# A fused dynamic convolution and two feed-forward blocks: the head of the program rebuilt, with small unread matmuls in planned waits

## The chip, the core and the metric

The kernel runs on one core of one Trainium2 chip. The metric is the device time of one execution in microseconds (us). A core has five engines with a queue each: PE (TensorE, matrix products into PSUM), ACT (ScalarE), DVE (VectorE), POOL (GpSimd, which has no access to PSUM here) and SP (SyncE, which issues all the DMAs of this kernel). PSUM has eight banks of 512 float32 columns.

## What is computed

The input x has 2 batches of 4160 tokens with 192 features. Three steps follow each other:

```python
w = softmax(weight_gen, axis=-1)                # (2, 4160, 8 heads, 7 taps)
att[b, s, h] = sum_k w[b, s, h, k] * x_pad[b, s + k, h]      # causal, 7 rows of x

xk, xr = mu_k * att + (1 - mu_k) * prev(att), mu_r * att + (1 - mu_r) * prev(att)
y = sigmoid(xr @ w_r) * (relu(xk @ w_k) ** 2 @ w_v)          # d_ff = 1024

h = relu(y @ w_in)
c = conv_w[0] * h[s - 1] + conv_w[1] * h[s] + conv_w[2] * h[s + 1]
out = (h * sigmoid(c)) @ w_out
```

Several weights arrive as float64 and are narrowed to float32 on the chip.

## The kernel before, in words

**Tiles.** Each batch is cut into ten tiles of tokens: 256, 220, seven of 476, and 352. The two batches (b0, b1) of a tile are worked side by side. Everything below runs per tile i and batch b.

**Stages of a tile.** `attention` (line 468) loads overlapping rows of x with one DMA per batch, multiplies 7 rows by the softmax weights in one 128x1344 product per token slot (2 slots per batch in tiles 0 and 1, 4 in the full ones), and sums the seven parts: with PE into a `pa` bank in tile 0 (`total`, line 486), with three POOL adds in the others. All these products run on POOL. The sums go to `tok`. `mixing` (line 509) transposes `tok` on PE and makes xk and xr, each as a high and a low part. Unit u=0 makes features 0 to 127 of b0, u=1 those of b1, and u=2 the remaining 64 features of both batches at once; u=2 sends its parts to `xB` by eight DMAs from SBUF to SBUF (lines 567, 568) and needs both batches. `moe1` (line 608) makes one of eight 128-wide chunks of the first block: five matmuls into a `pa` bank, ReLU, square and a cast on ACT, a subtraction on DVE, and later five more matmuls (`out_passes`) into the accumulators `am` and `ar`. `gate_r` makes the sigmoid gate, `mix_out` multiplies by it and writes `x2`. `moe2` does the second block in the same manner (`pc` bank, tapped convolution on ACT and DVE, accumulators `bm` and `br`), 12 steps behind `moe1`; tiles 0 and 1 are handled together in it, as one unit of 476 tokens.

**Weights.** `prepare` (line 416) fetches sixteen chunks of weights through a ring of three `stage` buffers and narrows each (`narrow`, line 337): an ACT copy with a scale into bank `bm` or `br`, four DVE instructions, two matmuls that add the float32 parts, and then a split into high and low parts by two ACT casts with a matmul between. The narrowed value and its power of two use two rings of banks, `px_r` (`bm`, `br`) and `py_r` (the two `pc` banks).

**Softmax.** Tile 0, tile 1, tile 2 and the rest are four groups (`softmax`, line 437): DVE reduces and inverts, ACT takes the exponential, and the two broadcast passes (subtract the maximum, multiply by the inverse) run on DVE for tile 0 and on POOL for the others.

**Order.** Every instruction is first recorded with a planned time `now` (`at(t, ...)`), which is a priority. `Program.schedule` (line 114) then goes through all of them with a table of costs (`cost`, line 84), always gives the next free engine the ready instruction with the lowest `now`, and emits everything in the order of the planned starts. Each engine's queue is in that order on the chip; waits between engines are by semaphores on the real data. SP's queue is planned in the same way, and a DMA whose buffer isn't free holds up the DMAs behind it. `hold` is a planned time before which an instruction isn't placed: the row loads of tile 1 have 25.0 and 33.0.

Of the kernel before, what the change touches and what calls it, by code (L numbers as in the profile page):

```python
# [16 lines left out]
SIZES = [256, 220] + [476] * 7 + [352]  # L17
# [25 lines left out]
class Program:  # L43
# [40 lines left out]
    def cost(self, eng, method, out, ins, pointer):  # L84
# [3 lines left out]
        if method == "dma_start":  # L88
            return 0.6, 0.0
# [24 lines left out]
    def schedule(self):  # L114
# [4 lines left out]
        for i, (eng, method, a, k, _, hold) in enumerate(self.ops):  # L119
# [38 lines left out]
        for _ in range(n):  # L158
# [39 lines left out]
def conv_moe_kernel(ctx: ExitStack, tc: tile.TileContext, xp, wg_first, wg_rest, mus, w_k, w_v, w_r, w_in, conv_w, w_out, out):  # L198
# [90 lines left out]
    py_r = Ring(pc_r.tiles)  # L289
# [5 lines left out]
    omt_r = Grow(om_r.tiles, (SPARE, [spare[:, 5 * W:6 * W]]))  # L295
    pt_r = Grow(pc_r.tiles, (16 * NTILE, pa_r.tiles))
# [40 lines left out]
    def narrow(st, n):  # L337
# [5 lines left out]
        ACT.activation(px, f(hi), ACTF.Copy, scale=2.0 ** -112)  # L343
        if on_pe[0]:

            zr = wz_r()[:, :n]
            DVE.tensor_scalar(x, x, 3, None, op0=ALU.logical_shift_left)
            DVE.scalar_tensor_tensor(out=z, in0=hi, scalar=0x80000000, in1=x, op0=ALU.bitwise_and, op1=ALU.bitwise_or)
# [4 lines left out]
            return px  # L353
        DVE.tensor_scalar(x, x, 3, None, op0=ALU.logical_shift_left)
# [82 lines left out]
    def softmax(j, a, b, eng, times, bank):  # L437
# [3 lines left out]
        if bank is not None:  # L441
            z = bank[:, :n * NH].rearrange("p (s h) -> p s h", s=n)
# [25 lines left out]
    def attention(i, b, t_load, t, dt_, eng, hold=(0.0, 0.0)):  # L468
# [7 lines left out]
        def token(l):  # L476
# [7 lines left out]
            if i < 1:  # L484

                def total():
# [3 lines left out]
                    ACT.copy(tok_t[i][:, l, b * DM:b * DM + DM], z)  # L490
# [18 lines left out]
    def mixing(i, u, t, dt_):  # L509
# [5 lines left out]
        def flip():  # L515
# [408 lines left out]
```

## Time and profile before

| | |
|---|---|
| median of 3 runs | 742.6 us (742.06 to 743.72) |
| the profiled execution, its own time | 743.48 us |
| its span in the profile | 741.7 us, so 1.8 us lie outside the span |
| busy share: PE, weight loads, ACT, DVE, POOL | 96%, 82%, 88%, 78%, 74% |
| granted TensorE clock, mean | 0.992 of full speed |

Times in the rows are in us from the start of the span unless marked ns; PEld is PE's loading of weights, SPq SP's queue. All recorded instructions carry line 183, where the schedule emits them, so they are told apart by the names of their tiles: `prod` is a product of the convolution, `pa` the bank of a first matmul, `s` the hidden values, `am` and `ar` the accumulators, `stage` raw weights (and, late, scratch), `sw` the softmax weights.

### The profile page before, as it was taken

The page shows a single profiled execution, that of the slowest core. Times are in us where ns is not written, and L with a number is a line of the kernel's source. Part 1 is how long each engine was busy: PE and PEld are TensorE (multiplying, and loading weights), DVE is VectorE, ACT ScalarE, POOL GpSimd, SP SyncE. Part 2 cuts the span into 40 slices and gives each one's busy share as a digit, 9 for nine tenths or more (in the row PEclk, how much of TensorE's full clock was granted, in tenths as well). Part 3 has the DMA queues.
Part 4 walks back from the last instruction along what each step waited for, and adds up shares of the span by engine and source line. Part 5 has one row for each costly group of instructions (what it writes and reads, how often), then busy time and mean ns, then how long its engine had stood idle before and what let it go on. Part 6 is the DMA issues. An engine that isn't in the chain of part 4 may idle for free.

```text
span 741.7 us, 10552 instructions
## 1 busy us (share of the span) xinstructions
PE 708.9 (96%) x3473; PEld 606.4 (82%) x3473; DVE 579.6 (78%) x985; ACT 653.6 (88%) x1388; POOL 547.0 (74%) x398
## 2 busy tenths in 40 slices
PE   3898988999999999999999999999999999999996
PEld 2776777888788888888888888888888888899995
DVE  5666977888898978797879787978796858686775
ACT  2588788999999999898989898989898989899986
POOL 3798999999799999999999999999013423242333
PEclk9899999999999999999999999999999999999999
DMA  7678203021310230212112302120002000200000
GB/s 223 172 219 258 97 1 106 1 74 53 73 54 20 82 93 7 73 47 81 53 27 74 101 1 68 61 61 1 20 5 69 0 21 0 60 2 21 1 21 30
DMA packets 18791, 45.09 MB, mean 61 GB/s; under 512 B 2992, under 2 KB 14256, under 8 KB 18608
## 3 DMA queue, kind: packets, MB, share of 16 engines
q1 hardware_dynamic: 18736, 44.41, 20.1%
q8 instruction: 27, 0.44, 0.3%
q14 instruction: 28, 0.23, 0.1%
HBM read 27.40 MB, written 6.39 MB: 46 GB/s over the span
## 4 chain that ended last, share of the span: by engine, by line
PE 80%; POOL 8%; ACT 5%; issue 3%; DVE 2%; DMA 1%; SPq 0%; POOLq 0%; ACTq 0%; DVEq 0%
PE pa L183 25%; PE pc L183 18%; PE bm L183 12%; PE am L183 11%; PE br L183 7%; PE ar L183 7%; POOL prod L183 5%; ACT pa L183 1%; DMA stage<-in_moe_w_k_dram 1%; POOL s L183 1%; ACT L183 1%; DVE stage L183 0%; POOL g L183 0%; POOL xA L183 0%; POOL tok L183 0%
## 5 line engine op out<-in xcount | busy, mean ns | idle before, releaser
L183 DVE SCALAR_TENSOR_TENSOR pc<-h,cw,pc 128x476 f32<-128x476 f32 (+1 forms) x276 | 194.4, 704 | 42.2 <-ACT pc L183 39.3
L183 POOL TENSOR_TENSOR prod<-rows,sw 128x1344 f32<-128x1344 f32 x70 | 216.5, 3094 | 13.5 <-DMA stage<-in_moe_w_v_dram 10.9
L183 ACT ACTIVATE pa<-pa 128x476 f32<-128x476 f32 (+4 forms) x326 | 163.9, 504 | 38.0 <-PE pa L183 33.6
L183 POOL TENSOR_TENSOR prod<-prod 128x576 f32<-128x576 f32 (+1 forms) x132 | 161.5, 1224 | 9.6
L183 PE MATMUL am<-s,wv 128*128 128x476 f32 (+3 forms) x480 | 141.8, 356 | 0.9 <-ACT s L183 0.9
L183 PE MATMUL bm<-g,wo 128*128 128x476 f32 (+1 forms) x411 | 133.6, 379 | 1.1 <-ACT g L183 0.8
L183 PE MATMUL pa<-xA,wkA 128*128 128x476 f32 (+3 forms) x480 | 123.6, 363 | 5.2 <-DVE ar L183 2.5
L183 POOL TENSOR_TENSOR g<-stage,g 128x476 fp32r<-128x476 f32 (+1 forms) x41 | 47.5, 1158 | 97.5 <-ACT g L183 93.6
L183 DVE TENSOR_TENSOR s<-pa,s 128x476 fp32r<-128x476 f32 (+3 forms) x160 | 93.9, 587 | 27.8 <-ACT s L183 27.1
L183 PE MATMUL pc<-x,wiA 128*128 128x478 f32 (+1 forms) x414 | 112.0, 376 | 0.0
L183 PE MATMUL ar<-s,wv 128*128 128x476 f32 (+3 forms) x320 | 108.9, 354 | 0.2 <-DVE x L183 0.2
L183 PE MATMUL br<-g,wo 128*128 128x476 f32 (+1 forms) x274 | 102.3, 375 | 0.0
L183 PEld LDWEIGHTS pa<-xA,wkA 128*128 128x128 f32 x480 | 83.4, 190 | 23.1 <-DVE s L183 6.7
L183 PEld LDWEIGHTS am<-s,wv 128*128 128x128 f32 x480 | 86.8, 188 | 12.8 <-ACT s L183 2.1
L183 ACT ACTIVATE pc<-h,cw 128x476 f32<-128x476 f32 (+1 forms) x138 | 92.0, 667 | 1.2
L183 PE MATMUL pa<-xB,wkB 128*128 128x476 f32 (+3 forms) x320 | 88.7, 357 | 0.0
L183 PEld LDWEIGHTS bm<-g,wo 128*128 128x128 f32 x411 | 76.2, 189 | 12.6 <-ACT g L183 1.6
L183 DVE TENSOR_TENSOR pc<-h,pc 128x476 f32<-128x476 f32 x96 | 62.8, 654 | 29.8 <-ACT pc L183 29.4
L183 PEld LDWEIGHTS pc<-x,wiA 128*128 128x128 f32 x414 | 75.6, 189 | 11.8 <-DVE g L183 2.0
L183 ACT CAST s<-pa 128x476 fp32r<-128x476 f32 (+3 forms) x160 | 82.3, 516 | 1.9
L183 ACT ACTIVATE h<-pc 128x478 f32<-128x478 f32 (+1 forms) x138 | 78.9, 572 | 5.5 <-PE pc L183 4.5
L183 PE MATMUL pc<-x,wiB 128*128 128x478 f32 (+1 forms) x276 | 81.4, 375 | 0.0
(147 smaller groups left out, 1170.6 us busy)
## 6 DMA issues: line engine op xcount, KB each, us to landing
rows<-in_x_dram SPq DMA_DIRECT2D x14, 960.0 KB, 4.7
xB<-rm SPq DMA_DIRECT2D x28, 119.0 KB, 2.3
rows<-in_x_dram SPq DMA_DIRECT2D x4, 768.0 KB, 6.9
xB<-mk SPq DMA_DIRECT2D x16, 119.0 KB, 2.3
rows<-in_x_dram SPq DMA_DIRECT2D x2, 864.0 KB, 4.4
out_dram<-stage SPq DMA_DIRECT2D x7, 238.0 KB, 2.0
out_dram<-om SPq DMA_DIRECT2D x7, 238.0 KB, 2.2
stage<-in_moe_w_v_dram SPq DMA_DIRECT2D x4, 384.0 KB, 4.3
```

Source lines behind the costliest of these rows:

```text
L183: getattr(self.real[eng], method)(*a, **k)
```

## The change

Only the head, up to the first full tile, is rebuilt; tiles 2 to 9 keep their code.

1. Tiles 0 and 1 become 238 tokens each instead of 256 and 220, so two chunks of one tile fit side by side in one bank (2 x 238 = 476 columns). `moe1_half`, `gate_half` and `mix_out_half` do for tiles 0 and 1 two chunks (or both feature halves) in one instruction on ACT and DVE. The matmuls stay one per chunk and pass.
2. In tile 0 the two products of b0 move from POOL to DVE, with an earlier time; those of b1 stay on POOL. The softmax of tile 1 and tile 2 moves from POOL to DVE, that of tile 1 before the weights; the maximum and the sum of the first three groups are kept in bank `am`.
3. `tok` of tile 0 also holds the last 64 features twice (one more ACT copy per slot). New mixing units 5 and 6, one per batch, transpose that doubled block and write `xB` in place, so unit 2 and its eight DMAs go in tile 0, and b0 no longer waits for b1.
4. `narrow` gets its sign from a parametric ReLU on ACT instead of an AND/OR on DVE: three DVE instructions instead of four, in all sixteen chunks.
5. `py_r` has one bank; the other `pc` bank is lent to the `pa` ring (three banks) up to planned time 26.
6. The plan prices a DMA's issue at 0.45 us (0.6 before), its bandwidth at 310 GB/s (240), its landing at 0.75 us (0.8), and takes the exponential's table as loaded. The row loads of tile 1 are held to 8.0 and 16.0 instead of 25.0 and 33.0.
7. Where PE waits in the plan between 2.5 and 48.0 us, the schedule puts 32-column matmuls (signs times signs) into columns 480 to 511 of bank `am`, one per 0.11 us of planned wait, until 0.15 us before the next real matmul. Nobody reads them.

```diff
-SIZES = [256, 220] + [476] * 7 + [352]
+SIZES = [238, 238] + [476] * 7 + [352]
+WARM = 2.5, 48.0
@@ cost / schedule
-            return 0.6, 0.0
+            return 0.45, 0.0
...
+        done = WARM[0]
         for i in sorted(range(n), key=lambda i: (start[i], i)):
             eng, method, a, k = self.ops[i][:4]
+            if eng == "PE":
+                while done < start[i] - 0.15 and start[i] < WARM[1]:
+                    self.idle(done == WARM[0])
+                    done += 0.11
+                done = start[i] + dur[i]
             getattr(self.real[eng], method)(*a, **k)
@@ banks
-    py_r = Ring(pc_r.tiles)
+    py_r = Ring(pc_r.tiles[:1])
...
+    LENT = 26
+    pa_r = Lend(LENT, pa_r.tiles + pc_r.tiles[1:], pa_r)
@@ narrow
-        ACT.activation(px, f(hi), ACTF.Copy, scale=2.0 ** -112)
...
-            DVE.tensor_scalar(x, x, 3, None, op0=ALU.logical_shift_left)
-            DVE.scalar_tensor_tensor(out=z, in0=hi, scalar=0x80000000, in1=x, op0=ALU.bitwise_and, op1=ALU.bitwise_or)
+            ACT.activation(px, f(hi), ACTF.Prelu, scale=2.0 ** -112, alpha=-(2.0 ** 32))
+            DVE.tensor_scalar(z, x, 3, None, op0=ALU.logical_shift_left)
@@ softmax
-            z = bank[:, :n * NH].rearrange("p (s h) -> p s h", s=n)
+            m, z = (bank[:, k * n * NH:(k + 1) * n * NH].rearrange("p (s h) -> p s h", s=n) for k in (0, 1))
@@ attention, tile 0
-                    ACT.copy(tok_t[i][:, l, b * DM:b * DM + DM], z)
+                    x = tok_t[i][:, :, b * DM:b * DM + DM]
+                    m, r = 64 * b, 128 - 128 * b
+                    ACT.copy(x[:, l, m:m + 128], z[:, m:m + 128])
+                    ACT.copy(x[:, L + l, 0:128].rearrange("p (k d) -> p k d", k=2), z[:, r:r + 64].unsqueeze(1).to_broadcast([128, 2, 64]))
@@ mixing
+            elif u > 4:
+                x = xB_r[k]()
+                xin[i, u - 5, k, 1] = x
+                x = x.unsqueeze(1)
...
+            if u > 4:
+                h = slice(64, 128)
+                (POOL if i else DVE).tensor_tensor(x[h, 0, :N], st[k][h, :N], f(x[h, 0, :N]), op=ALU.subtract)
+                return
@@ moe1_half (gate_half and mix_out_half are built alike)
+        def go():
+            st["p"] = pa_r()[:, :2 * N]
+            for j, p in enumerate(halves(st["p"], N)):
+                mm(p, passes_in(wkA, wkB, xin[i, b, 0, 0], xin[i, b, 0, 1], slice(128 * (fi + j), 128 * (fi + j) + 128), N))
+        def c1():
+            ACT.activation(st["p"], st["p"], ACTF.Relu)
...
+        def go2():
+            m, r = halves(HALF[b], N)
+            for j in range(2):
+                out_passes(wv, fi + j, st["s"][:, :, j * N:j * N + N], N, m, r, one=True)
@@ the plan
-    attention(0, 0, -100.1, -90, 0.1, POOL)
+    attention(0, 0, -100.1, -94.3, 0.05, DVE)
...
-    softmax(1, 0, slots[1], POOL, (-83.85, -83.65, -83.64, -83.63, -83.62, -83.55), am_r.tiles[0])
+    softmax(1, 0, slots[1], DVE, (-92, -91.9, -91.8, -91.7, -91.6, -91.5), am_r.tiles[0])
...
-    softmax(2, 0, slots[2], POOL, (0.9, 0.91, 0.92, 0.93, 0.94, 0.95), None)
+    softmax(2, 0, slots[2], DVE, (0.9, 0.91, 0.92, 0.93, 0.94, 0.95), am_r.tiles[0])
...
-    mixing(0, 2, -75, 0.1)
-    mixing(0, 1, -70, 0.1)
+    mixing(0, 5, -87, 0.1)
+    mixing(0, 1, -75, 0.1)
+    mixing(0, 6, -74, 0.1)
...
+    prog.idle = lambda first: nc.tensor.matmul(am_r.tiles[0][:, 480:512], lhsT=signs[:, 0:128], rhs=signs[:, 0:32], start=first, stop=True, skip_group_check=True)
```

## Rows read from the trace of the kernel before

**Rows 1.** Busy time of each engine by stretches, granted clock, DMA:

```profile
core 0: us, PE busy (x) PEld busy (x) DVE busy (x) ACT busy (x) POOL busy (x), PEclk, DMA share, GB/s
11.20:32.00 20.80, 19.08 (x79) 14.65 (x79) 14.06 (x29) 8.78 (x24) 15.53 (x8) 1.00 0.71 193
32.00:60.00 28.00, 23.24 (x123) 17.89 (x124) 20.43 (x43) 22.42 (x65) 24.94 (x19) 0.88 0.68 207
60.00:80.00 20.00, 17.61 (x112) 14.05 (x112) 13.18 (x33) 16.10 (x49) 17.96 (x15) 1.00 0.72 208
80.00:100.00 20.00, 17.32 (x127) 15.25 (x126) 17.06 (x35) 16.25 (x58) 19.37 (x14) 1.00 0.14 51
100.00:124.80 24.80, 21.37 (x128) 17.99 (x126) 19.65 (x34) 21.33 (x45) 22.92 (x19) 1.00 0.20 60
124.80:130.00 5.20, 5.20 (x17) 4.42 (x18) 3.25 (x7) 4.45 (x11) 5.04 (x4) 0.67 0.43 94
200.00:273.00 73.00, 73.00 (x343) 61.98 (x343) 65.16 (x109) 68.35 (x139) 70.49 (x48) 1.00 0.17 51
...
32.00:40.00 8.00, 5.59 (x16) 3.68 (x16) 7.08 (x17) 5.49 (x17) 7.76 (x6) 0.57 0.35 84
```

**Rows 2.** The timeline of PE, first complete chunk of tile 2:

```profile
124.78 1.34 PE L183 MATMUL pa<-xA,wkA 128*128 128x476 f32 x3 [0.44 <-ACT r L183]
```

**Rows 3.** The timeline of POOL: start, us, instruction, idle before:

```profile
12.29 6.04 POOL L183 TENSOR_TENSOR prod<-rows,sw 128x1344 f32<-128x1344 f32 x2 [10.94 <-DMA stage<-in_moe_w_v_dram]
...
32.02 3.03 POOL L183 TENSOR_TENSOR prod<-rows,sw 128x1344 f32<-128x1344 f32 x1
...
114.76 2.37 POOL L183 TENSOR_TENSOR xA<-stage,xA 128x476 fp32r<-128x476 f32 x2
```

**Rows 4.** The timeline of DVE around the first softmax:

```profile
5.21 0.55 DVE L183 TENSOR_REDUCE h<-sw 128x32 f32<-128x224 f32 x1 [4.32 <-DMA sw<-in_first_dram]
...
7.01 0.56 DVE L183 TENSOR_REDUCE am<-sw 128x32 f32<-128x224 f32 x1 [0.46 <-ACT sw L183]
...
10.25 0.19 DVE L183 TENSOR_SCALAR am<-am 128x32 f32<-128x32 f32 x1
...
10.98 0.35 DVE L183 RECIPROCAL h<-am 128x32 f32<-128x32 f32 x1
...
11.83 0.37 DVE L183 TENSOR_TENSOR sw<-sw,h 128x224 f32<-128x224 f32 x1
```

**Rows 5.** SP's queue: row loads of tile 0's b1 and tile 1's b0:

```profile
3.97 0.43 SPq L183 DMA_DIRECT2D rows<-in_x_dram  x1
...
21.40 1.21 SPq L183 DMA_DIRECT2D rows<-in_x_dram  x1
```

**Rows 6.** DMA issues, count, KB each, median us to landing:

```profile
rows<-in_x_dram SPq DMA_DIRECT2D x4, 768.0 KB, 6.9
```

**Rows 7.** Groups of instructions up to 200 us on ACT: busy, mean ns of one:

```profile
L183 ACT ACTIVATE pa<-pa 128x476 f32<-128x476 f32 x36 | 19.8, 556 | 1.1 <-PE pa L183 0.8
L183 ACT ACTIVATE pa<-pa 128x256 f32<-128x256 f32 x32 | 12.1, 383 | 4.9 <-PE pa L183 4.6
L183 ACT ACTIVATE pa<-pa 128x220 f32<-128x220 f32 x32 | 11.0, 344 | 3.9 <-PE pa L183 3.5
```

**Rows 8.** Groups of DVE instructions, the same view over the whole span:

```profile
L183 DVE TENSOR_TENSOR g<-pc,g 128x476 fp32r<-128x476 f32 x96 | 62.3, 649 | 10.7 <-ACT g L183 10.6
...
L183 DVE SCALAR_TENSOR_TENSOR stage<-stage,br 128x384 uint32<-128x384 uint32 x5 | 2.7, 549 | 0.1
```

**Rows 9.** Two equal DVE instructions, and what POOL ran beside the second:

```profile
29.93 0.20 DVE L183 TENSOR_SCALAR h<-h 128x64 f32<-128x64 f32 x1
...
192.66 0.71 DVE L183 TENSOR_SCALAR stage<-stage 128x64 f32<-128x64 f32 x1
...
192.12 1.20 POOL L183 TENSOR_TENSOR stage<-stage,rm 128x476 fp32r<-128x476 f32 x1
```

**Rows 10.** The timeline of ACT, one of its four table loads up to 125 us:

```profile
52.78 1.28 ACT L183 ACT_TABLE_LOAD   x1
```

More of the change, by code (lines that the diff above doesn't have):

```diff
@@ L33 @@
 S_LAG, G_LAG = 3.25, 4.75
+S_LAG_HALF, HSTEP = 3.25, 1
+HEAD = {(i, b): 16 * i + 8 * b for i in range(2) for b in range(2)}
 DONE = 16 * NTILE + S_LAG - 0.95
@@ L174, in schedule @@
                 wires[eng] = max(wires[eng], t + dur[i] + 0.6) + moved[i]
-                end = wires[eng] + 0.8
+                end = wires[eng] + 0.75
             for j in succ[i]:
@@ L295, in conv_moe_kernel, with __init__, __call__ @@
     omt_r = Grow(om_r.tiles, (SPARE, [spare[:, 5 * W:6 * W]]))
+    class Lend:
+        def __init__(self, until, first, then):
+            self.until, self.first, self.then = until, Ring(first), then
+        def __call__(self):
+            return self.first() if prog.now < self.until else self.then()
+    LENT = 26
+    pa_r = Lend(LENT, pa_r.tiles + pc_r.tiles[1:], pa_r)
+    pa_r.tiles = pa_r.then.tiles
     pt_r = Grow(pc_r.tiles, (16 * NTILE, pa_r.tiles))
@@ L582, in conv_moe_kernel @@
     r_t = {}
+    HALF = [am_r.tiles[0], ar_r.tiles[0]]
     acc = {}
@@ L644, in moe1, with halves, gate_half, sg @@
         at(t + S_LAG, go2)
-    def out_passes(W, fi, s, n, am, ar):
+    def halves(bank, n):
+        return bank[:, 0:n], bank[:, n:2 * n]
+    def gate_half(i, b, t):
+        N = SIZES[i]
+        st = {}
+        def go():
+            st["p"] = pa_r()[:, :2 * N]
+            for k, p in enumerate(halves(st["p"], N)):
+                mm(p, passes_in(wrA, wrB, xin[i, b, 1, 0], xin[i, b, 1, 1], slice(128 * k, 128 * k + 128), N))
+        def sg():
+            r_t[b, "half"] = r_r[b]()[:, :2 * N]
+            ACT.activation(r_t[b, "half"], st["p"], ACTF.Sigmoid)
+        at(t, go)
+        at(t + 0.3, sg)
@@ new lines, in mix_out_half, with d0, a0, d2 @@
+    def mix_out_half(i, b, t):
+        N = SIZES[i]
+        X = x2[b]
+        c = slice(OFFSET[i] + 2, OFFSET[i] + N + 2)
+        both = HALF[b][:, :2 * N]
+        m, r = halves(both, N)
+        def d0():
+            DVE.tensor_tensor(both, r_t[b, "half"], both, op=ALU.mult)
+        def a0():
+            ACT.copy(X[0:64, 3, c], r[0:64])
+            ACT.copy(X[:, 0:3:2, c], both.rearrange("p (k n) -> p k n", k=2))
+        def d2():
+            DVE.tensor_tensor(X[64:128, 3, c], r[0:64], f(X[0:64, 2, c]), op=ALU.subtract)
+            DVE.tensor_tensor(X[:, 1, c], m, f(X[:, 0, c]), op=ALU.subtract)
+        at(t, d0)
+        at(t + 0.15, a0)
+        at(t + 0.4, d2)
@@ L843, in conv_moe_kernel @@
             carry(i, b, t + 7)
-            for k in range(2):
-                gate_r(i, b, k, t + 5.12 + k)
-            for fi in range(NF):
-                moe1(i, b, fi, t + fi)
-                if i:
+            if i < 2:
+                h = HEAD[i, b]
+                gate_half(i, b, h + 5.12 * HSTEP)
+                for fi in range(0, NF, 2):
+                    moe1_half(i, b, fi, h + HSTEP * fi)
+                mix_out_half(i, b, h + S_LAG_HALF + 6 * HSTEP + 0.27)
+            else:
+                for k in range(2):
+                    gate_r(i, b, k, t + 5.12 + k)
+                for fi in range(NF):
+                    moe1(i, b, fi, t + fi)
+                mix_out(i, b, t + S_LAG + 7.27)
+            if i:
+                for fi in range(NF):
                     moe2(i, b, fi, t + fi + LAG)
-            mix_out(i, b, t + S_LAG + 7.27)
             if i:
```

46 lines of the change are left out of this document (34 added, 12 removed).

## The prediction

> **What bounds the kernel now.** I read the busy times by stretches first. From 200 to 273 us PE is busy for all 73.00 of 73 us [rows 1], and the page's slices say the same up to the last one. Past about 130 us the end is therefore set by PE's queue alone: a microsecond of PE's idle time that is saved earlier comes off the end, and nothing else does. Before that PE waits. It begins at 11.2 us, and from there to 124.8 us its busy time falls short of the span in every stretch: by 1.7, 4.8, 2.4, 2.7 and 3.4 us, 15.0 us together [rows 1]. There are hidden losses too: from 32 to 40 us the granted clock is 0.57, so a good part of these 8 us went at the lower of the two levels (1.2 instead of 2.4 GHz), with PE busy for only 5.59 of them; and from 80 to 100 us PE handled 127 matmuls against 128 in the following 24.8 us, of which many are twice as wide [rows 1], so short matmuls stand apart there.
>
> Next, who holds PE up. The chain of waits lies on POOL's products without a break until tile 2 is summed, and POOL's timeline tells why: its first product starts at 12.29, tile 1's first at 32.02, and the last sum of tile 2 is done when its subtraction starts at 114.76 [rows 3]. From there it is 10.0 us of mixing, casts and DMAs to the first complete chunk of tile 2 on PE at 124.78 [rows 2]. After that PE waits for POOL no more: its busy time is full although POOL's own, 70.49 of 73, is not [rows 1].
>
> **The change part by part.**
>
> *POOL's start.* Between 12.29 and 32.02 POOL did four products of tile 0 and the softmax passes of tiles 1 and 2. Two products and the four passes leave it. What remains is two products at 3.02 us, half of the 6.04 of the pair [rows 3], so 6.0 us. They need the softmax and b1's rows. The softmax of tile 0 starts at 5.21 and has its sum at 7.57; the three instructions left (0.19, 0.35, 0.37 us) ended only at 12.20, since the weight chunk's shifts stood between them [rows 4]. With the softmax first they end at about 7.57 + 0.91 + three gaps of 0.1 = 8.8. The rows of b1 were issued at 3.97 [rows 5] and land after about 6.9 [rows 6], at 10.9.
>
> *The products of b0 on DVE.* No row shows a 128x1344 product there. Of tensor-tensor instructions on DVE, 224 columns take 0.37 [rows 4] and 476 take 0.65 us [rows 8], so 1.1 ns a column and about 1.6 us for 1344; POOL's 3.02 is the upper bound. I take 1.6: done at 8.8 + 3.2 = 12.0. DVE and POOL read SBUF at once then, and a row bears on it: the same 128x64 instruction took 0.20 us with POOL idle and 0.71 us when a POOL subtraction ran from 192.12 to 193.32, and it ended as that ended [rows 9].
>
> By that row POOL's first product of b1 waits for DVE's second, to 12.0 instead of 10.9, or DVE's second waits up to 3.0 us for POOL. The Trainium skill ("SBUF — State Buffer", "Who interferes with whom") says that a VectorE instruction with two SBUF inputs and a GpSimd instruction that reads SBUF exclude each other for whole instructions; by that rule POOL starts at 12.0, without it at 10.9. The softmax passes that move have their second input in PSUM, so only these two products are concerned.
>
> I take 12.0, and POOL is free at 18.0. Tile 1 also needs its own softmax, seven instructions like those above, 3 to 4 us once its weights are there, so about 16, and its rows. Their load was issued at 21.40 [rows 5]; with the smaller hold it can go when b0's products free the buffer at 12.0, and lands by 12.4 + 6.9 = 19.3 at the latest, 17 if the wires are free. I take 18.5 for tile 1's first product instead of 32.02: **13.5 us earlier**. Bounds: 17.0 (no lock, rows in time) gives 15; if the load isn't issued before 21.40 since SP stands at a weight fetch whose buffer is taken, it lands at 28 and the gain is 4. Loads that go earlier pass in front of the fetches of w_k and w_v and of the copies to wkB, which lose the wire time of one row load, 3 to 4 us; these chunks are needed when the products' mixing is through, some 25 us, so they have room.
>
> *POOL from tile 1 to tile 2.* Nothing else changes on POOL: 82.7 us from 32.02 to 114.76, of which some 4 are waits. Tile 2 is then summed at 101.2, and its first chunk can start at 111.3 if the 10.0 us behind it stay.
>
> *Can the others keep up?* PE must have done by 111.3 what it had done by 124.8. That has to come out of its idle 15.0 us and the clock; so ACT, DVE and the banks decide. For tiles 0 and 1 ACT did 32 chunks, with two passes and a cast each: 48 instructions of 0.383 and 48 of 0.344 [rows 7], 34.9 us. It now does 16 pairs with three at 0.556, 26.7 us: 8.2 less. Gates and `mix_out` save 1 to 2 us more. Eight added instructions in tile 0 (copies, shifts, casts) cost at most 8 x 0.38 = 3.1. The parametric ReLU replaces a copy one for one. ACT's 84.9 us from 11.2 to 124.8 become about 78, in 100 us: 78%, against 94% from 200 to 273 us [rows 1]. DVE loses nine sign instructions of 0.55 us [rows 8] and six wider ones, 9 us in all, saves 3 on the pairs, and gets 3.2 for products, 2 for softmax passes and 2 for the fourth mixing unit: 5 us less. A pair holds its bank for one round of ACT and DVE where two chunks had two, and there are three banks at first. The matmuls stay as many, with as many columns. SP loses eight DMAs, and b0 of tile 0 no longer waits for b1's products, so `moe1` of tile 0 starts earlier. So I cost the pace at nothing; the cover is ACT's free 22%.
>
> *The unread matmuls.* In planned waits they cost nothing, and PE's queue is in order, so they run while the wait for real data goes on. Below: the stretch from 32 to 40 us at 0.57 [rows 1] lost up to 8 x 0.43 = 3.4 us, and a chain that passes through it is shortened by some of that. Above: of the 11.2 us before PE's first matmul 8.7 lie behind 2.5, and some 4 more of waits follow up to 48 us; at 0.11 us each that is about 115 matmuls, 12.7 us, if all of them fell on work. I take zero, the nearer end, as the waits are waits for others. The stretch at 0.67 from 124.8 to 130 us [rows 1] lies beyond them.
>
> *Sum.* The profiled execution took 743.5 us, 0.9 above the median of the runs shown. 743.5 - 13.5 = 730.0; against the median 742.6 it is **729.1 us**.
>
> **The rivals.**
>
> *The pace binds (0.18).* POOL is early, but the narrowing of sixteen chunks, two banks at a time, and ACT hold PE. For it: ACT was busy 80% and more from 32 to 60 us [rows 1] with PE waiting. Against it: the ACT and DVE savings above. Then only the slow clock's 3.4 us and some 3 us of bank waits go: 736.
>
> *More than POOL's shift (0.14).* Pairs also close the idle 3.4 us before 124.8, 2.7 of 80 to 100, and 1.7 of the slow 5.2 us behind it [rows 1]: 13.5 + 7.8, so 721.3.
>
> *No change (0.06).* The row load stays late and PE's idle time only moves: 742.
>
> *The unread matmuls tie PE to DVE (0.08), slower.* They write bank `am`, in which the first three softmax groups now keep their maxima and sums, and their place in the queues is that of the plan, whose DMA prices are lower than the 6.9 us of the rows [rows 6]. If a matmul that waits for late weights stands ahead of them, every softmax instruction on that bank waits behind it on DVE, and POOL behind that. With softmax 1 done at 23 instead of 16, 6.5 us are lost, and with all 12.7 us on work: 729.1 + 19.2 = 748.3. It decides from 13.5 us of such losses on.
>
> *The parametric ReLU needs a table of its own (0.03), slower.* No row shows the function. A load takes 1.28 us [rows 10]; to and fro for sixteen chunks is 32 loads, 41 us, of which ACT's idle time up to 100 us hides 25 and its savings 7; with POOL's gain lost, 743.5 + 9 = 752. The Trainium skill ("ScalarE: Activation LUTs", "Table sets: the hidden batching unit") says that cheap functions are in every set as filler, and doesn't name this one; by it there are no loads.
>
> **How the numbers follow.** The forecast has 0.51. About 0.2% (1.5 us) is what a measurement of this kernel can tell from no change. Faster by more: 0.51 + 0.18 + 0.14 = 0.83; within: 0.06; slower: 0.08 + 0.03 = 0.11. The forecast's own bounds (gains of 4 and 15) give 727.6 to 738.6. The range takes in both faster rivals and half of no change, 717 to 742, which leaves out the slower cases and a tail below, under 0.2.
>
> **What would show it.** Right: POOL's first product of tile 1 at 17 to 20 us, the last of tile 2 done by 99 to 103, first complete 476-column chunk on PE at 109 to 113; two DVE products of about 1.6 us before 13 us; table loads still four up to that chunk; ACT's hidden-layer passes 476 wide; granted clock at 1.00 from 30 to 48 us. Wrong: the row load of tile 1 still issued past 20 us; POOL early but PE idle in front of ACT; softmax instructions on DVE that wait for PE; or PE's real matmuls queued behind unread ones.

## The result and the profile after

The changed kernel takes **749.5 us** (median of 5 runs, 748.91 to 754.32) beside 742.6 us of the kernel before (741.96 to 744.3): a ratio of 1.0111, 95% interval 1.0091 to 1.0131. The forecast was 729.1 us, within 717 to 742. So the sign is wrong, and the distance is 20.4 us. The profiled execution of the changed kernel is its longest run, 754.32 us; a second one, near the median, comes with the experiments (e12).

Busy time by stretches, as in [rows 1], of the changed kernel, whose span is 752.5 us:

```profile
core 0: us, PE busy (x) PEld busy (x) DVE busy (x) ACT busy (x) POOL busy (x), PEclk, DMA share, GB/s
0.00:11.20 11.20, 5.13 (x25) 5.17 (x25) 6.14 (x12) 3.45 (x6) 0.75 (x7) 1.00 0.80 247
11.20:32.00 20.80, 20.23 (x95) 18.23 (x96) 11.88 (x26) 8.52 (x26) 11.06 (x5) 1.00 0.54 180
32.00:60.00 28.00, 26.51 (x161) 22.29 (x162) 20.07 (x39) 20.87 (x55) 22.95 (x17) 0.88 0.58 185
60.00:80.00 20.00, 16.32 (x112) 13.79 (x112) 10.31 (x23) 14.59 (x37) 14.68 (x13) 0.95 0.78 220
80.00:100.00 20.00, 19.28 (x141) 18.46 (x140) 15.85 (x26) 16.27 (x41) 18.05 (x13) 0.88 0.20 70
100.00:124.80 24.80, 18.65 (x97) 15.75 (x97) 17.15 (x28) 15.62 (x30) 20.57 (x16) 0.93 0.11 41
200.00:273.00 73.00, 69.15 (x315) 58.13 (x315) 62.98 (x105) 62.45 (x128) 66.31 (x45) 0.98 0.19 54
```

PE is busier than before up to 60 us, 51.9 of 60 instead of 42.3 (13.9 us of it are unread matmuls), and yet no further: it falls short by 3.7 us from 60 to 80 (2.4 before), by 6.2 from 100 to 124.8 (3.4 before), and by 3.9 from 200 to 273, where the kernel before lost nothing.

The timeline of PE at the start; line L979 is the unread matmul, L194 the list schedule that issues everything else:

```profile
6.07 8.26 PE L979 MATMUL am<-signs 128*128 128x32 f32 x38 [6.07 <-DVE sw L194]
14.16 7.63 PE L194 MATMUL pa<-prod,ident 128*128 128x192 f32 x28
```

The first 38 unread matmuls stand in front of the first sums of tile 0's products. They can't begin before DVE's softmax has left bank `am`, at 6.07, and they take 8.26 us, 0.217 each where the plan prices 0.11. The 28 sums behind them then take 7.63 us: the first 18 start 0.32 us apart, the last ten 0.16. In the same trace and those of the experiments 14 of these sums take 2.44 us, 0.17 each, when they run later. So 8 us of 32-column matmuls haven't brought PE to the faster pace. It begins at 19.9 us, where the trace's first record of the granted clock stands, at the higher of the two levels (2.4 instead of 1.2 GHz); before that record the PEclk column reads 1.00 only because nothing is recorded.

The group of the unread matmuls in the whole span, busy time, mean ns of one, and idle time before them:

```profile
L979 PE MATMUL am<-signs 128*128 128x32 f32 x80 | 15.1, 326 | 8.1 <-DVE sw L194 6.4 <-DVE am L194 1.7
```

The timeline of DVE in the first 27 us:

```profile
5.53 0.39 DVE L194 TENSOR_TENSOR sw<-sw,am 128x224 f32<-128x224 f32 x1
...
7.69 3.03 DVE L194 TENSOR_TENSOR prod<-rows,sw 128x1344 f32<-128x1344 f32 x2
...
14.36 0.56 DVE L194 TENSOR_REDUCE am<-sw 128x32 f32<-128x224 f32 x1 [0.39 <-PE am L979]
...
23.40 0.47 DVE L194 SCALAR_TENSOR_TENSOR ar<-pc,mu,att 128x238 f32<-128x238 f32 x1 [7.60 <-ACT att L194]
...
26.07 0.38 DVE L194 TENSOR_TENSOR sw<-sw,am 128x224 f32<-128x224 f32 x1
```

Softmax 0 is done at 5.92 and the two products of b0 at 10.7. Softmax 1 begins at 14.36 but ends only at 26.45: from 15.8 on its sum stands behind a mixing instruction (`ar`), which waits 7.60 us for ACT, which waits for the sums on PE. The exponential that the softmax's sum needs stands on ACT behind the copies of the same PE sums, too, and runs only at 23.27.

The timeline of POOL, as in [rows 3]:

```profile
19.08 6.04 POOL L194 TENSOR_TENSOR prod<-rows,sw 128x1344 f32<-128x1344 f32 x2 [17.73 <-PE pa L194]
26.83 3.04 POOL L194 TENSOR_TENSOR prod<-rows,sw 128x1344 f32<-128x1344 f32 x1 [1.71 <-PE pa L194]
...
56.21 0.69 POOL L194 TENSOR_TENSOR xA<-mk,xA 128x238 fp32r<-128x238 f32 x1 [4.27 <-ACT xA L194]
...
116.68 2.37 POOL L194 TENSOR_TENSOR xA<-stage,xA 128x476 fp32r<-128x476 f32 x2
```

There are two product buffers. DVE fills both, and POOL's first product waits until PE has summed one: 19.08, not 12.29. Tile 1's first product comes 5.2 us earlier than before, and all of it is given back on the way to tile 2, which is summed at 116.68 instead of 114.76.

### The profile page after: what moved, and what is told of

Same layout as the page of the kernel before. It is cut to its first block, busy times and chain, and to the rows that moved or that the text cites. A ratio compares the mean times of both kernels' runs of the same rounds, so it can differ in the third digit from the quotient of the medians.

```text
span 752.5 us, 10602 instructions
## 1 busy us (share of the span) xinstructions
PE 721.4 (96%) x3555; PEld 624.2 (83%) x3555; DVE 578.7 (77%) x959; ACT 649.2 (86%) x1340; POOL 537.6 (71%) x392
## 4 chain that ended last, share of the span: by engine, by line
PE 86%; ACT 5%; DVE 3%; issue 2%; POOL 1%; DMA 1%; POOLq 0%; ACTq 0%; DVEq 0%
PE pa L194 26%; PE pc L194 19%; PE bm L194 12%; PE am L194 12%; PE br L194 8%; PE ar L194 8%; PE am L979 2%; DVE stage L194 1%; POOL s L194 1%; ACT pc L194 1%; ACT pa L194 1%; ACT x L194 1%; DVE pc L194 1%; DVE am L194 1%; DMA stage<-in_moe_w_out_dram 1%
## 5 line engine op out<-in xcount | busy, mean ns | idle before, releaser
L194 DVE SCALAR_TENSOR_TENSOR pc<-h,cw,pc 128x476 f32<-128x476 f32 (+1 forms) x276 | 194.4, 705 | 45.3 <-ACT pc L194 42.4
L194 POOL TENSOR_TENSOR prod<-rows,sw 128x1344 f32<-128x1344 f32 x68 | 210.2, 3091 | 19.8 <-PE pa L194 19.4
L194 ACT ACTIVATE pa<-pa 128x476 f32<-128x476 f32 (+2 forms) x284 | 153.2, 540 | 32.2 <-PE pa L194 28.3
L194 POOL TENSOR_TENSOR prod<-prod 128x576 f32<-128x576 f32 (+1 forms) x132 | 161.5, 1224 | 9.3
L194 PE MATMUL bm<-g,wo 128*128 128x476 f32 (+1 forms) x411 | 134.7, 379 | 7.5 <-ACT g L194 7.2
L194 PE MATMUL am<-s,wv 128*128 128x476 f32 (+2 forms) x464 | 134.1, 357 | 0.0
L194 PE MATMUL pa<-xA,wkA 128*128 128x476 f32 (+2 forms) x450 | 119.4, 370 | 0.6 <-ACT r L194 0.4
L194 POOL TENSOR_TENSOR g<-stage,g 128x476 fp32r<-128x476 f32 (+1 forms) x41 | 47.5, 1159 | 97.5 <-ACT g L194 93.6
L194 PE MATMUL pc<-x,wiA 128*128 128x478 f32 (+1 forms) x414 | 113.5, 380 | 0.7 <-ACT x L194 0.7
L194 PE MATMUL ar<-s,wv 128*128 128x476 f32 (+2 forms) x336 | 106.1, 355 | 2.9 <-ACT s L194 2.8
L194 PE MATMUL br<-g,wo 128*128 128x476 f32 (+1 forms) x274 | 103.3, 378 | 2.1 <-DVE stage L194 2.1
L194 DVE TENSOR_TENSOR s<-pa,s 128x476 fp32r<-128x476 f32 (+1 forms) x139 | 88.2, 634 | 17.9 <-ACT s L194 17.4
L194 PEld LDWEIGHTS pa<-xA,wkA 128*128 128x128 f32 x450 | 81.0, 193 | 17.0 <-DVE s L194 3.0
L194 ACT ACTIVATE pc<-h,cw 128x476 f32<-128x476 f32 (+1 forms) x138 | 92.1, 668 | 1.3
L194 PEld LDWEIGHTS bm<-g,wo 128*128 128x128 f32 x411 | 76.7, 189 | 19.3 <-ACT g L194 8.6
L194 PEld LDWEIGHTS am<-s,wv 128*128 128x128 f32 x464 | 81.8, 189 | 10.3 <-DVE x L194 0.3
L194 ACT ACTIVATE h<-pc 128x478 f32<-128x478 f32 (+1 forms) x138 | 79.0, 572 | 13.1 <-PE pc L194 12.2
L194 PEld LDWEIGHTS pc<-x,wiA 128*128 128x128 f32 x414 | 76.0, 190 | 13.2 <-DVE g L194 2.7
L194 DVE TENSOR_TENSOR pc<-h,pc 128x476 f32<-128x476 f32 x96 | 62.7, 653 | 31.5 <-ACT pc L194 31.3
L194 ACT ACTIVATE pc<-pc 128x476 f32<-128x476 f32 (+1 forms) x148 | 81.1, 548 | 5.3 <-DVE pc L194 2.3
L194 PE MATMUL pa<-xB,wkB 128*128 128x476 f32 (+2 forms) x300 | 85.2, 364 | 0.0
L194 PE MATMUL pc<-x,wiB 128*128 128x478 f32 (+1 forms) x276 | 81.7, 376 | 0.0
```

## The experiments

All times are medians; the kernel before took 742.3 to 742.7 us beside them. The ledger that the experiments lead to is the sum PE busy + PE idle = span, from the first line of each profile. The spans are those of the profiled executions, which lie up to 1.4 us off the medians beside them (e9 above its median by that much), so differences of 1 us between rows say little:

| kernel | time, us | span | PE busy | of it unread | idle | tile 2 summed on POOL |
|---|---|---|---|---|---|---|
| before | 742.6 | 741.7 | 708.9 | 0 | 32.8 | 114.76 |
| e9, front alone | 741.6 | 741.2 | 707.6 | 0 | 33.6 | 106.30 |
| e3, all but unread matmuls and prices | 736.1 | 733.7 | 706.6 | 0 | 27.1 | 104.14 |
| e1, all but unread matmuls | 738.9 | 737.1 | 703.0 | 0 | 34.1 | 105.00 |
| e12, the changed kernel | 748.5 | 746.7 | 717.4 | 15.7 | 29.3 | 114.66 |
| e13, e3 with 34 unread matmuls | 735.4 | 733.1 | 705.8 | 6.0 | 27.3 | 105.80 |

### e1: no unread matmuls

```diff
-WARM = 2.5, 48.0
+WARM = 2.5, 0.0
```

> The changed kernel without its unread matmuls; order and everything else as it is. Theory A (the 80 unread matmuls hold up PE's queue in the head: the first 38 ran from 6.07 to 14.3 us at 0.217 us each, though the first product was there at about 9.2): PE's first product sum starts at 9 to 10 us, POOL's first product at 13 to 15 instead of 19.08, POOL's first product of tile 1 at 20 to 22 instead of 26.83, and the time falls by 5 to 12 us, to 737 to 744. Rival B (the new order as such is what the chip does badly, with DVE, ACT and POOL queues that wait in the wrong place): the time stays at 746 or more, and POOL still waits some 10 us in tiles 1 and 2.

738.88 us (736.32 to 739.31), ratio 0.9947, interval 0.9933 to 0.996. Its first product sum and its POOL:

```profile
8.32 6.84 PE L194 MATMUL pa<-prod,ident 128*128 128x192 f32 x28 [8.32 <-DVE prod L194]
```

```profile
12.98 6.05 POOL L194 TENSOR_TENSOR prod<-rows,sw 128x1344 f32<-128x1344 f32 x2 [11.62 <-DMA stage<-in_moe_w_v_dram]
20.19 3.06 POOL L194 TENSOR_TENSOR prod<-rows,sw 128x1344 f32<-128x1344 f32 x1 [1.16 <-PE pa L194]
...
105.00 2.38 POOL L194 TENSOR_TENSOR xA<-stage,xA 128x476 fp32r<-128x476 f32 x2
```

The unread matmuls cost 749.5 - 738.9 = 10.6 us and make the sign. Without them the sums start 5.8 us earlier and POOL is where the prediction had it within 2 to 4 us: tile 1 at 20.2 (forecast 18.5), tile 2 summed at 105.0 (forecast 101.2), 9.8 earlier than before. But the time is only 3.4 us shorter than the 742.29 beside it. That is the second question.

### e2: unread matmuls in the kernel before

```diff
+WARM = 2.5, 48.0
...
+            if eng == "PE":
+                while done < start[i] - 0.15 and start[i] < WARM[1]:
+                    self.idle(done == WARM[0])
+                    done += 0.11
```

> The kernel before with the same rule for unread matmuls in its own planned waits up to 48 us (its plan gives 146 of them, 71 ahead of the first real matmul), nothing else changed. Theory A: 71 x 0.217 us can't all fit before 11.2 us, PE's first real matmul comes 5 to 15 us later, and the time rises by 5 to 15 us, to 748 to 758. Rival B: they run in real waits and cost under 3 us, 741 to 746.

762.55 us (762.31 to 763.42), ratio 1.0271, interval 1.0255 to 1.0287: 20.3 us, more than the 5 to 15 expected. The timeline of PE:

```profile
11.21 15.30 PE L867 MATMUL am<-signs 128*128 128x32 f32 x71 [11.21 <-DVE h L191]
26.35 2.05 PE L191 MATMUL bm<-stage,ident 128*128 128x512 f32 x2
```

Here 71 of 146 stand in front of the first real matmul, which starts at 26.35 instead of 11.2, 15.1 of the 20.3 us. They take the planned wait twice: once while they wait for DVE themselves, and once again as work.

### e3: the old prices in the plan, no unread matmuls

```diff
-            return 0.45, 0.0
+            return 0.6, 0.0
...
-        port, table = 0.0, ACTF.Exp
+        port, table = 0.0, None
```

(and a DMA's 310e3 back to 240e3, 0.75 to 0.8, and `WARM` as in e1).

> The changed kernel without its unread matmuls and with the old prices of DMAs and the exponential's table in the plan (0.6, 240, 0.8, not loaded). It differs from the run without unread matmuls only in the order of the queues. If the new prices matter, it is over 3 us off that run, slower if they are nearer to the chip; if they don't, within 2 us of it.

736.09 us (735.72 to 738.03), ratio 0.9921, interval 0.9907 to 0.9934. By the medians the new prices are 2.8 us worse than the old, not better; that lies between the two expectations, and the intervals of e1 and e3 just touch. POOL is as early in both (104.14 and 105.00), and the difference lies behind it: from 140 to 300 us PE is busy for 155.3 of 160 in e1 and for 159.7 in e3. The largest single loss of e1 there is seen on three engines, PE, DVE and POOL:

```profile
201.01 0.92 PE L194 MATMUL ar<-s,wv 128*128 128x476 f32 x3 [2.48 <-DVE x L194]
...
197.30 2.98 DVE L194 TENSOR_SCALAR stage<-stage 128x64 f32<-128x64 f32 x1
...
197.17 3.06 POOL L194 TENSOR_TENSOR prod<-rows,sw 128x1344 f32<-128x1344 f32 x1
```

A small DVE instruction, 0.20 us with POOL idle [rows 9], starts 0.13 us after one of POOL's products and takes 2.98 us, to 0.05 us after the product's end. The instruction behind it on DVE is late, and PE waits 2.48 us for that. The Trainium skill ("SBUF — State Buffer", "Who interferes with whom") calls the port that the two engines share an exclusive lock; this row agrees, with 2.98 us beside 0.20. An order that meets or misses such a collision is worth microseconds, and no step of the prediction looked for one there.

### e4: wide unread matmuls

```diff
-nc.tensor.matmul(am_r.tiles[0][:, 480:512], lhsT=signs[:, 0:128], rhs=signs[:, 0:32], ...
+nc.tensor.matmul(am_r.tiles[0][:, 256:512], lhsT=signs[:, 0:128], rhs=signs[:, 0:256], ...
```

(only in waits planned before 25 us.)

> The changed kernel with unread matmuls of 256 instead of 32 columns, up to 25 us of the plan instead of 48. If a matmul's place costs what its weight load costs (0.217 us at the slow pace), the first 38 take 8.3 us as before; if wide ones raise the clock earlier, they take less, and the 28 matmuls of the first sums take 4.9 us instead of 7.6. Then 2 to 5 us less than the changed kernel, 744 to 747. If neither, the same as the changed kernel, 749 to 751.

741.7 us (738.2 to 745.95), ratio 0.9992, interval 0.9974 to 1.001. The timeline of PE:

```profile
5.91 6.67 PE L979 MATMUL am<-signs 128*128 128x256 f32 x38 [5.91 <-DVE sw L194]
12.42 4.71 PE L194 MATMUL pa<-prod,ident 128*128 128x192 f32 x28
```

38 matmuls of 256 columns take 6.67 us where 38 of 32 columns took 8.26, and the 28 sums behind them 4.71 instead of 7.63, 0.17 each. Up to 10.1 us the wide ones start 0.21 us apart, as the 32-column ones do; from there on it is 0.12, and the trace's first record of the granted clock stands at 10.20, where e1, without unread matmuls, has it at 12.49 and the changed kernel at 19.94. So in this run the idea of warming works, with wide matmuls, and the time is below the 744 to 747 that were expected for it. It still loses 2.8 us to none at all: POOL's first product comes at 14.95 instead of 12.98, and in the ledger PE is busy for 709.0 us, 6.0 more than in e1, and idle for 30.0, 4.1 less.

### e5 and e6: which of the 80, and which bank

```diff
# e5
-WARM = 2.5, 48.0
+WARM = 12.0, 48.0
-    prog.idle = lambda first: nc.tensor.matmul(am_r.tiles[0][:, 480:512], ..., start=first, ...
+    prog.idle = lambda first: nc.tensor.matmul(am_r.tiles[0][:, 480:512], ..., start=True, ...
# e6
-    prog.idle = lambda first: nc.tensor.matmul(am_r.tiles[0][:, 480:512], ...
+    prog.idle = lambda first: nc.tensor.matmul(ar_r.tiles[0][:, 480:512], ...
```

Both serve for timing alone: their outputs are wrong, presumably since the unread matmuls disturb the sums accumulated in the bank that they write. Instructions and shapes are those of the changed kernel.

> The changed kernel, its unread matmuls only in waits planned after 12 us: by the plan the 38 ahead of the first product sum go and about 42 stay. Theory A (the cost is the 38, which stand between the softmax on bank am and the first product sum and make POOL late): the first sum at 8 to 9 us, POOL's first product at 13, tile 1 at 20 to 22, the time 738 to 742. Theory B (each unread matmul costs wherever it stands): 42 of 80 of the 10.6 us, so 738.9 + 5.6 = 744.5.

> The changed kernel, all unread matmuls written to bank ar, which the early softmax doesn't use. Theory A1 (the tie through bank am is half of it: the 38 could not start before 6.07, when the softmax of tile 0 was through with the bank): they start at about 2.6, last 8.3 us, end at 10.9, the first product sum is at 11 instead of 14.2, and the time is some 3 us under 749.5, about 746. Theory A2 (the tie is all of it, since softmax 1 on DVE waits for them as well): first sum at 8 to 9, time 738 to 741. Theory A3 (the tie is nothing, the count is all): 749.

e5: 741.32 us (739.3 to 745.21), with 42 unread matmuls; its first sum at 8.38, tile 1 at 20.51. So by the medians the first 38 cost 8.2 of the 10.6 us and the other 42 cost 2.4: theory A, and not a price for each. The split is rough, as e5's runs lie 5.9 us apart; e12 shows where the other 42 cost something. e6: 748.24 us (744.8 to 750.74), ratio 1.0069, interval 1.0042 to 1.0096. Its timeline of PE:

```profile
2.38 8.29 PE L979 MATMUL ar<-signs 128*128 128x32 f32 x38 [2.38 <-ACT signs L194]
10.51 7.01 PE L194 MATMUL pa<-prod,ident 128*128 128x192 f32 x28
```

Free of the softmax's bank, the 38 start at 2.38 and the sums at 10.51 instead of 14.16; tile 1 starts at 22.55. The median gains 1.3 us, within the intervals of both. So the tie through `am` is at most a small part of what costs: A1's 3 us are at the edge of what was seen, A2's 8 are excluded. Of the 3.5 us that the first sum gains on e12 (10.51 and 14.05), 1.7 are lost again up to the matmul `br<-wv,signs` at 37.65 (39.48 in e12), since later unread matmuls now wait for bank `ar`.

### e7 and e8: the b0 products back on POOL, the sign back on DVE (both on e3)

```diff
# e7
-    attention(0, 0, -100.1, -94.3, 0.05, DVE)
+    attention(0, 0, -100.1, -94.3, 0.05, POOL)
# e8
-            ACT.activation(px, f(hi), ACTF.Prelu, scale=2.0 ** -112, alpha=-(2.0 ** 32))
-            DVE.tensor_scalar(z, x, 3, None, op0=ALU.logical_shift_left)
+            ACT.activation(px, f(hi), ACTF.Copy, scale=2.0 ** -112)
+            DVE.tensor_scalar(x, x, 3, None, op0=ALU.logical_shift_left)
+            DVE.scalar_tensor_tensor(out=z, in0=hi, scalar=0x80000000, in1=x, op0=ALU.bitwise_and, op1=ALU.bitwise_or)
```

> The fastest so far (old DMA prices, no unread matmuls, 736.1), with the two b0 products of tile 0 back on POOL, the softmax still first. As the prediction reckoned (two products of 3.02 us leave POOL's row): POOL is 6 us later from there, tile 1 at 26, time 741 to 742. Rival (POOL stood idle until 12.7 us for the rows of b1 anyway, and tile 1 waits for its softmax at 19.8 as well): POOL does b0 from 6.1 to 12.2 and b1 to 18.8, tile 1 at 20.8 to 22, time 736 to 738.

> The same kernel with the sign put on by DVE again instead of by the parametric ReLU on ACT, so with one more DVE instruction of 0.55 to 0.68 us per weight part. If DVE is not what binds the early part (the prediction's step): 735.5 to 737.5. If it binds: up to nine of them on the path, 5 to 6 us, 741 to 742.

e7: 741.75 us (740.42 to 743.31), 5.7 us over e3. The time is the one that the prediction's reckoning gives, but not by its way: tile 1 starts at 22.57, 1.8 us later than in e3 and not 6, since POOL had stood idle there; tile 2 is summed at 107.70, 3.6 later, and the first sums of tile 0 come at 12.86 instead of 7.80. e8: 739.67 us (739.35 to 740.51), 3.6 us over e3, while POOL is as early as there (20.86 and 104.26). So something other than POOL decides.

### e9 and e10: the front alone

The kernel before with the softmaxes on DVE and first, b0's products on DVE and the smaller hold, nothing else; e10 adds the parametric ReLU.

```diff
-    attention(0, 0, -100.1, -90, 0.1, POOL)
+    attention(0, 0, -100.1, -94.3, 0.05, DVE)
...
-    softmax(1, 0, slots[1], POOL, (-83.85, -83.65, -83.64, -83.63, -83.62, -83.55), am_r.tiles[0])
+    softmax(1, 0, slots[1], DVE, (-92, -91.9, -91.8, -91.7, -91.6, -91.5), am_r.tiles[0])
...
-attention(i, b, T - 22 + 4.5 * b, ..., 1.125, POOL, (25.0 + 8 * b if i == 1 else 0.0, 0.0))
+attention(i, b, T - 22 + 4.5 * b, ..., 1.125, POOL, (8.0 + 8 * b if i == 1 else 0.0, 0.0))
```

> The kernel before with the front part of the change alone: softmax first, the two b0 products on DVE, softmax 1 and 2 on DVE with maxima and sums in bank am, tile 1's rows held back less. No pairs, no doubled rows, no parametric ReLU, no unread matmuls, old prices. Theory A (the gain is POOL's earlier start, and PE takes it on without the pairs): POOL's first product of tile 1 at 19 to 22 us, tile 2 summed at 103 to 106, time 734 to 738. Theory B (without pairs ACT and DVE can't keep up, so the later stages give it back): POOL as early as that, first complete chunk of tile 2 at 119 or later, time 740 to 742.

> The same and the sign by the parametric ReLU on ACT. If DVE's early queue binds, as the 3.6 us of the run with the sign on DVE suggest, 2 to 4 us under the front part alone; if those 3.6 us belong to the pairs' order, no difference beyond 1 us.

e9: 741.63 us (741.18 to 743.04), ratio 0.9991, interval 0.9982 to 1.0001: hardly a gain. Its POOL and its PE at tile 2:

```profile
22.70 3.06 POOL L183 TENSOR_TENSOR prod<-rows,sw 128x1344 f32<-128x1344 f32 x1 [2.28 <-PE pa L183]
...
106.30 2.35 POOL L183 TENSOR_TENSOR xA<-stage,xA 128x476 fp32r<-128x476 f32 x2
```

```profile
116.80 0.93 PE L183 MATMUL pa<-xA,wkA 128*128 128x476 f32 x3 [1.07 <-ACT r L183]
117.56 0.60 PE L183 MATMUL pa<-xB,wkB 128*128 128x476 f32 x2
```

POOL is 8.5 us earlier, and the first chunk of tile 2 starts 8.0 us earlier than in [rows 2]: the chain from POOL to that chunk on which the forecast was built is there. The end has not moved. The first line of this profile and of the one before, busy time of each engine:

```profile
PE 707.6 (95%) x3473; PEld 606.0 (82%) x3473; DVE 586.5 (79%) x991; ACT 651.1 (88%) x1388; POOL 537.2 (72%) x392
```

```profile
PE 708.9 (96%) x3473; PEld 606.4 (82%) x3473; DVE 579.6 (78%) x985; ACT 653.6 (88%) x1388; POOL 547.0 (74%) x398
```

PE's idle time is 33.6 us of 741.2 and was 32.8 of 741.7. Up to 124.8 us PE is busy for 99.4 us in e9 and for 98.6 in the kernel before, with 568 and 562 matmuls: the first chunk of tile 2 mostly takes the place of other chunks, which come later. What PE waits for up to 140 us in e9 (total, times, longest):

```profile
PE pa L183 <- DVE prod L183: 9.8, 1, 9.8
PE am L183 <- ACT s L183: 4.1, 4, 1.9
PE bm L183 <- DVE stage L183: 3.4, 3, 1.2
PE pa L183 <- DVE s L183: 1.9, 4, 0.8
PE br L183 <- ACT wv L183: 1.9, 2, 1.2
```

Behind the first, which is the start, these are ACT's casts, DVE's subtractions and the weight chunks of both, and none is POOL: theory B, by the time and by what holds PE up. Its landmark, the chunk of tile 2 at 119 us or later, it missed. e10: 743.23 us (741.43 to 745.03), interval 1.0002 to 1.0024; the ReLU alone brings nothing here and is 1.6 us slower than e9. With the pairs, the equal tiles, the doubled rows and the third bank too (e3) PE has started 599 matmuls by 124.8 us, idle time falls to 27.1 us, and the end comes 7.5 us of span earlier than in e9 (5.5 by the medians), at nearly the same POOL (104.14).

### e11: old prices, unread matmuls kept

```diff
-            return 0.45, 0.0
+            return 0.6, 0.0
```

(with the other prices as in e3.)

> The changed kernel with the old prices of the plan, unread matmuls kept. If prices (2.8 us) and unread matmuls (10.6 us) add up: 736.1 + 10.6 = 746.7. The plan with higher DMA prices has longer waits, so more unread matmuls; if the count decides, it comes out above 749.5.

748.03 us (746.96 to 751.9), ratio 1.0089, interval 1.0056 to 1.0122. There are 114 unread matmuls, 21.0 us of them, 53 in front of the first sum at 17.64. It comes out between the two expectations: 12 us over e3, which is more than 10.6, but not over the changed kernel.

### e12: the changed kernel once more

> The changed kernel once more, for a profile nearer to its median, since the one shown is its longest run (754.32 of a median of 749.51). If the account of that profile is right (against the kernel without unread matmuls: 15.1 us of unread matmuls, some 3 us of real matmuls at the lower clock, less 3 us of idle time taken), a run of about 749.5 has the same 15.1 us, and either less at the lower clock or 5 us more of the idle time taken. First product sum at 14, tile 1 at 26 to 27, tile 2 summed at 113 to 117.

748.51 us (745.26 to 750.32), and a profile of that same time. Its first line and its POOL:

```profile
PE 717.4 (96%) x3555; PEld 620.8 (83%) x3555; DVE 578.4 (77%) x959; ACT 648.7 (87%) x1340; POOL 537.7 (72%) x392
```

```profile
25.70 3.05 POOL L194 TENSOR_TENSOR prod<-rows,sw 128x1344 f32<-128x1344 f32 x1 [1.17 <-PE pa L194]
...
114.66 2.38 POOL L194 TENSOR_TENSOR xA<-stage,xA 128x476 fp32r<-128x476 f32 x2
```

Against e1, all in the ledger: PE is busy for 14.4 us more. The unread matmuls take 15.7 us, of which 2.0 overlap real ones; the real ones by themselves take 703.7 us instead of 703.0, so the clock gives nothing back. Idle time falls by 4.8, from 34.1 to 29.3. 14.4 - 4.8 = 9.6, the difference of the spans. Less than a third of the unread matmuls' time fell into waits.

Both kernels issue the same 3475 real matmuls in the same order, so equal ones can be compared, and that shows where the 9.6 us arise. The first sum is 5.7 us later than in e1 (14.05 and 8.32), and the lag is still 5.7 at 31 us. Then unread matmuls stand in front of two matmuls that narrow a chunk of `w_v`:

```profile
35.36 1.68 PE L979 MATMUL am<-signs 128*128 128x32 f32 x7 [0.86 <-DVE am L194]
...
37.75 1.89 PE L979 MATMUL am<-signs 128*128 128x32 f32 x8 [0.31 <-DVE sw L194]
39.48 0.46 PE L194 MATMUL br<-wv,signs 128*128 128x128 f32 x1
```

In e1 the last of these starts at 29.97 after a wait of 0.63 us, here 9.5 us later. Behind that the lag moves up and down, and at the end it is 9.6. POOL sums tile 2 at the same time as in the kernel before (114.66 and 114.76), though the span is 5.0 us longer: POOL does not tell the end.

### e13: fewer unread matmuls, at their measured price (on e3)

```diff
-WARM = 2.5, 0.0
+WARM = 12.0, 48.0
-        done = WARM[0]
+        done, first = WARM[0], True
-                    self.idle(done == WARM[0])
-                    done += 0.11
+                    self.idle(first)
+                    done, first = done + 0.22, False
```

> The fastest so far (old prices, no unread matmuls, 736.1) with unread matmuls only in waits planned after 12 us, and priced in the plan at the 0.217 us that the trace shows instead of 0.11, so about half as many per wait. If unread matmuls can pay by the clock: the granted clock of 30 to 40 us above the 0.68 without them, time 733 to 735.5. If planned waits aren't the waits of the chip: 737 to 740, POOL's waits for xA longer than 3.3 us.

735.43 us (733.2 to 735.8), ratio 0.9899, interval 0.9882 to 0.9917: the fastest of all, 7.3 us under the kernel before, though its interval overlaps that of e3, so a gain over e3 isn't shown. The group and the clock from 30 to 40 us:

```profile
L979 PE MATMUL am<-signs 128*128 128x32 f32 x34 | 6.0, 258 | 2.0 <-DVE am L194 1.5 <-DVE sw L194 0.5
```

```profile
30.00:40.00 10.00, 8.88 (x47) 0.79 0.78 245
```

The clock is granted at 0.79 there and at 0.68 in e3, above it as expected, but that comes of the stretch chosen: PE is at the lower level from 33.5 to 40.4 us in e3 and from 35.9 to 42.7 in e13, equally long, and from 33 to 45 us the clock is 0.72 in both. In the ledger against e3: the unread matmuls take 6.0 us, of which 3.4 overlap real ones; the real ones take 3.4 less (703.2 and 706.6); idle time is 0.2 more. In these two profiles the matmuls pay for themselves, but a gain by the clock isn't shown to be their doing: from 100 to 120 us, far behind them, the clock is 1.00 in e13 and 0.83 in e3.

## Why the prediction was wrong

The 20.4 us between forecast and result are three steps: 736.1 - 729.1 = **7.0** for a gain that was sized by POOL, 738.9 - 736.1 = **2.8** for the prices, 749.5 - 738.9 = **10.6** for the unread matmuls. The last makes the sign. The shares depend on the order in which the steps are taken: with the unread matmuls kept, the prices are worth 1.5 us (e11), which the intervals don't tell from nothing.

- *"The unread matmuls … I take zero."* This step failed: the term was put at nothing and measured 10.6 us. The bounds were right, the choice between them was not. "The waits are waits for others" holds for a wait of the chip; but these are issued in the plan's waits. The plan has the first sum at about 6.8 us (38 matmuls of 0.11 us behind 2.5) and fills the time before it; on the chip the softmax, not PE, sets when they may start, and they stand in front of work that is ready at about 8. At 0.217 us instead of 0.11 they also take twice what the plan thought; 0.11 is their pace at the higher level of the clock, at which five in a row run at 32 us in e12. Others stand in front of the matmuls of `w_v` in the same way (3.8 us in e12). The upper bound was reckoned with the plan's own price, so 80 of them came close to the 12.7 us that 115 were to cost. The lower bound's reason, the slow stretch from 32 to 40 us, gave nothing back: the real matmuls took 703.7 us with the unread ones and 703.0 without, and the clock from 30 to 48 us, forecast at 1.00, was 0.72 in e12.
- *POOL's start, 18.5.* DVE's two products took 1.5 us each, as worked out from its other rows, softmax 0 was done at 5.92 (forecast 8.8), and the row load of tile 1 was issued at 10.75, as the smaller hold was to bring. Two waits were left out: the product buffers are two, so POOL's products wait for PE's sums; and softmax 1, put at 16, ends at 19.8 even in e1, its exponential behind the copies of tile 0's sums on ACT and its sum behind a mixing instruction on DVE. That made 20.2 to 20.8 without the unread matmuls.
- *82.7 us from tile 1 to tile 2.* Right where PE isn't burdened: 83.3 in e3, 84.8 in e1. In the changed kernel 89.9, with 7.8 us of POOL's waits for ACT's `xA` instead of 3.2 in e1.
- *"I cost the pace at nothing."* This step failed too, though it did not turn the sign: e1 and e3 are faster than the kernel before. The first paragraph of the prediction said that only PE's idle time comes off the end; the sum was then taken along POOL to the first chunk of tile 2, on the condition that PE has done by 111.3 us what it had done by 124.8. Counted in real matmuls started (562 by then in the kernel before; their widths differ), e9 is there at 123.1 us, e3 at 117.2 and e1 at 112.8. e9, which lacks the pairs that the step counted on, has 8.5 us of POOL's shift and gains 0.8 us; e3 has 10.6 and gains 6.2. In e1 the pace nearly came out up to there, but little of it reached the end: from 140 to 300 us PE then lost 4.7 us, where the kernel before lost 0.4. ACT's free 22% was a mean; the waits of e9 are single ones for ACT and DVE between chunks. The rival in which the pace binds gave 736, and e3 took 736.1. That is near by luck in part: the rival counted on the 3.4 us of the slow clock, and e3 is at the lower level for as long as the kernel before (6.8 us from 33.5 on); it gains 5.7 us of idle time and 2.3 of busy time.
- *The rival in which the unread matmuls tie PE to DVE,* 748.3, came within 1.2 us, by its second half. They did wait for `am` and softmax 1 waited 0.39 us for them, but another bank changed little (e6); the work in front of the sums did the rest, and softmax 1 ended at 26.4 by the wait for those sums. That the number is so near is luck: the 6.5 us that it gave to the softmax stand where the 9.8 us of the other two steps belong.
- *The prices of the plan* were only read as "lower than the rows" and got no term. In e1 they gave an order that loses 4.3 us more from 140 to 300 us.
- *The parametric ReLU.* Right: no table load, and the price of the copy that it replaces. The timeline of ACT:

```profile
0.73 1.28 ACT L194 ACT_TABLE_LOAD   x1 [0.73 <-PEq L1034]
...
9.44 0.64 ACT L194 ACTIVATE bm<-stage 128x512 f32<-128x512 f32 x1 [5.16 <-DMA stage<-in_moe_w_k_dram]
```

  The next load comes at 58.89, for another function. The Trainium skill ("ScalarE: Activation LUTs", "Table sets: the hidden batching unit") has cheap functions in every set, and this one behaves so. Its saving on DVE was counted as cover and is worth 3.6 us in e3's order, nothing in e9's, where it comes out 1.6 us slower.
- *The lock between DVE and POOL* was put on the two first products. In none of these runs did they overlap, so it wasn't tried there; it showed at 197 us instead.

What stays open: why one order loses 3 to 4 us more than another from 140 to 300 us is shown for one wait of e1 only, and the share of the single parts of the pairs (width, third bank, doubled rows) wasn't tried.

## What to carry to other kernels

Where PE bounds the end, sum what PE does and what it waits for; that another engine reaches a landmark earlier is no gain until PE's idle time in the whole span is smaller. Work that is put into a planned wait is free only if it can start when the real wait starts and ends before the real work is ready, so price it from a trace, leave room, and look at what stands right behind it in the queue. A bank or a pair of buffers that an early step now shares is a new edge in the order: follow it to the engine that frees it.

## What the runs showed of the hardware

At the lower level of the clock an unread matmul with 32 columns of moving data started every 0.213 us, and so did one of 256 columns; at the higher level it was every 0.11 and 0.12 us. Each has a weight load of its own in the trace (80 beside 80). The first record of the granted clock, where the pace of equal matmuls doubles, stood at 10.20 us while 38 wide ones ran (from 5.91 on); 38 narrow ones up to 14.2 us in the changed kernel, and 71 from 11.2 to 26.4 us in e2, ended without it (19.94 and 37.74). This is one profile of each. And a 128x64 instruction of DVE took 2.98 us beside a product of POOL, fifteen times its 0.20.
